# Tile 3 of the first block normalised and turned by DMA instead of TensorE, with the D-skip row and block 2 loaded later

## The chip, the cores and the metric

The kernel runs on one core of a Trainium2 chip. A core has TensorE (PE, matrix products into PSUM), VectorE (DVE), ScalarE (ACT), GpSimd (POOL), and SyncE (SP), which here only issues DMAs. Each engine works through its own list of instructions in order, and semaphores tie the lists together. DMAs issued by one engine form a queue; ACT issues a few as well. The metric is the device time of one execution in microseconds, lower is better.

## The reference

For x of 2048 rows and 512 columns (bf16), the reference computes a normalisation and adds two branches to x:

```
xn  = (x - mean(x)) / sqrt(var(x) + 1e-5)                 # per row
A   = 2 * Re(h C^T) + xn * Dskip,  h_t = Lam_bar * h_(t-1) + B_bar xn_t    # complex states, 512 of them
B   = (gelu(xn @ w_gate) * (xn @ w_up)) @ w_down          # 512 -> 1376 -> 512
out = x + A + B
```

## The kernel before

**Tiling.** The 2048 rows are four blocks of 512, each of four tiles of 128 rows. For a block the kernel normalises (LN), turns the normalised tiles so that the 512 columns lie on partitions (TR, one DMA transpose for a tile, into XNT), computes the hidden layer (GU, w_gate and w_up as stationary operands), the input of the states (BU), the recurrence on DVE (CHAIN, real scans after a rotation by cosine and sine tables), and the down projection with the states added (DN). SKIP makes xn * Dskip; it reads the normalised tile XN and the D-skip row DSKB. XN has eight places, so block 2's normalised tiles overwrite block 0's, behind SKIP(0).

**The start of block 0.** PE should not wait for four normalised and turned tiles, so the first 896 hidden columns of block 0 are computed in the other order: x turned as stationary operand, the weights moving. Tile by tile, x minus its mean (function cent for tiles 0 and 1, sub for 2 and 3) is turned by TensorE itself (cent_T: four transposes against an identity, evacuated by ACT into XC). Since the rows lie on partitions, the factor 1/sqrt(var) is applied in the evacuation: gelu with scale on ACT, product with scale on DVE (GT_evac). Units are pairs of a tile j and a column group u: FR = 0:256, 256:512, 512:768, 768:896, gate and up columns side by side in one PSUM bank. Tiles 0 to 2 with u = 0, 1 are accumulated in steps (GT_k), as the weights' first 512 columns arrive row block by row block; the other ten units, tile 3's four among them, are done whole (GT_mm), each four matmuls. The product H0 is turned by DMA later (H0_T). The last 480 columns go the usual way (GU(0, [7, 8, 9, 10]), the first of them in two halves, tiles 0 and 1, then 2 and 3); for that all four tiles are normalised again (norms) and turned by DMA (TR).

**Weights.** w_gate and w_up come in pieces: four row blocks of columns 0 to 512 (ld_wk), then columns 512 to 896 and 896 to 1376 as one DMA each (ld_w). A buffer list (WGc, WUc) gives one dependency for each piece; wdeps maps a group of 128 columns to its piece.

**Order.** PE and SP run in the order in which the program adds their operations. DVE, ACT and POOL are ordered by a list planner (Sched) from estimated durations, with some links that fix the order of two operations on one engine (order_behind; ch makes a chain of them). The first statistics of a later block come behind the last product of GT_evac on DVE. The SP queue is: loads of x and weights, the parameters' transpose (tr_par), TR of block 0, x of block 1, the two transposes of B (load_B, 3 us of issue each), in the same function the D-skip row and x of block 2, then TR of block 1, the transpose of block 0's last hidden columns, H0_T, TR of block 2, and so on.

**Waits named below.** GT_mm needs its weight pieces and its turned tile. GU(0) needs TR of block 0 and the weight tails. BU(1) begins with its first units in halves, which need tiles 0 and 1 of block 1. LN(2) needs x of block 2; SKIP(0) needs the D-skip row. DN(0) first adds the hidden layer of all four tiles, then the states, which need CHAIN(0) and C scaled on DVE (L595).

Of the kernel before, what the change touches and what calls it, by code (L numbers as in the profile page):

```python
# [9 lines left out]
ALU = mybir.AluOpType  # L10
# [351 lines left out]
def d_act(n, ptr=0): return 190.0 + 0.833 * n + 90.0 * ptr  # L362
# [3 lines left out]
def build(nc, ins, out):  # L366
    with ExitStack() as es:
        E = es.enter_context
        S = Sched(nc, es)
# [11 lines left out]
        assert WG.lo == 0 and WU.lo == WG.hi  # L381
        WGU = arena_t[:, 0:2 * KD * F].rearrange("p (w k f) -> p w k f", w=2, k=KD)
        WD = A.alloc("WD", [KF, D], BF16)
        FC = [(0, 512), (512, 896), (896, F)]
        WGc = [Buf("WGc%d" % i, "sbx", 10 * i, 10 * i + 1) for i in range(KD + 2)]
        WUc = [Buf("WUc%d" % i, "sbx", 100 + 10 * i, 101 + 10 * i) for i in range(KD + 2)]
        wdeps = lambda Wc, ft: Wc[0:KD] if ft < 4 else [Wc[KD + (ft > 6)]]
        WDc = [Buf("WDc%d" % i, "sbx", 200 + 10 * i, 201 + 10 * i) for i in range(2)]
        XNT_all = A.alloc("XNT", [NB, KD, TB_], BF16)
        XNT = ring(XNT_all, "XNT", NB)  # L390
# [97 lines left out]
            return S.dma(lambda e: e.dma_start(W.ap[:, k, f0:f1], src[128 * k:128 * (k + 1), f0:f1]),  # L488
                         256 * (f1 - f0), writes=[Wc[k]], tag="ld_w")

        def ld_w(W, Wc, src, n):
            f0, f1 = FC[n]
            return S.dma(lambda e: e.dma_start(W.ap[:, :, f0:f1], src[:, f0:f1].rearrange("(k p) f -> p k f", p=128)),
                         1024 * (f1 - f0), writes=[Wc[KD + n - 1]], tag="ld_w")

        def ld_x0(j, queue="sync", after=()):
            return S.dma(lambda e, j=j: e.dma_start(X[j].ap, x2[128 * j:128 * (j + 1), :]), 128 * 1024, writes=[X[j]], tag="ld_x0", queue=queue, after=after)  # L497
# [2 lines left out]
        for k in range(KD):  # L500
# [1 line left out]
                ld_x0(k)  # L502
            ld_wk(WG, WGc, ins["B_w_gate"], k)
            ld_wk(WU, WUc, ins["B_w_up"], k)
        ld_w(WG, WGc, ins["B_w_gate"], 1)
        ld_w(WU, WUc, ins["B_w_up"], 1)

        def load_par():
            for q, nm in enumerate(("A_log_dt", "A_Lambda_re", "A_Lambda_im")):
# [14 lines left out]
        def load_T(bufs, nms):  # L524
            for b_, nm in zip(bufs, nms):
                S.dma(lambda e, b_=b_, nm=nm: e.dma_start_transpose(b_.ap, ins[nm]),
                      1.4 * 512 * 1024, writes=[b_], tag="tr_" + nm, issue=3000.0)

        def load_W():
            ld_w(WG, WGc, ins["B_w_gate"], 2)  # L530
            ld_w(WU, WUc, ins["B_w_up"], 2)

        def load_B():
            load_T([A.sub(BBT_all, "BBTc%d" % c, c) for c in range(2)], ("A_B_re", "A_B_im"))
            S.dma(lambda e: e.dma_start(DSKB.ap, ins["A_Dskip"].unsqueeze(0).broadcast_to([128, D])),
                  128 * 1024, writes=[DSKB], tag="ld_dsk")
            ld_x(2)
# [166 lines left out]
        def GT_mm(j, u, bank):  # L704
            f0, f1 = FR[u]
            w = f1 - f0
            dst = PS[bank][:, 0:2 * w].rearrange("p (w f) -> p w f", w=2)

            def f(e):
                ins_ = None  # L710
                for k in range(KD):
                    ins_ = e.matmul(dst, XCd(j, k), WGU[:, :, k, f0:f1], start=(k == 0), stop=(k == KD - 1))  # L712
                return ins_
            PE(f, d_pe([2 * w] * KD), wdeps(WGc, 2 * u) + wdeps(WUc, 2 * u) + XCs[j], [BANK[bank]], "GT")

        def GT_evac(j, u, bank):
            f0, f1 = FR[u]
            w = f1 - f0
            GATE["nh"] = kk = (GATE["nh"] + 1) % 3
            sc, rb = rss[j]  # L720
            GATE["last_gelu"] = S.order_behind(ACT(lambda e: e.activation(GG[kk].ap[:, 0:w], PS[bank][:, 0:w], ACTF.Gelu_apprx_tanh, scale=sc),  # L721
                                                   d_act(w, 1), [BANK[bank], rb], [GG[kk]], "gelu"), GATE.get("last_gelu"))
            hp = Buf("H0_%d_%d" % (j, u), "sb", H0[j].lo + 2 * f0, H0[j].lo + 2 * f1)
            GATE["hm"] = S.order_behind(V(lambda e: e.scalar_tensor_tensor(H0[j].ap[:, f0:f1], PS[bank][:, w:2 * w], sc, GG[kk].ap[:, 0:w], ALU.mult, ALU.mult),  # L724
                                          d_dve_1x(w), [BANK[bank], GG[kk], rb], [hp], "hmul"), GATE.get("hm"))

        def H0_T():
            for j in range(4):
# [77 lines left out]
        def GU_rest(b):  # L806
            k2, ft = b % 2, KF - 1
            f0, m = 128 * ft, FROWS[ft]
            for i in range(2):
                bank = next_bank()  # L810

                def f(e, i=i, bank=bank):
                    ins_ = None
                    for j in (2 * i, 2 * i + 1):
                        dst = PS[bank][:, 256 * (j % 2):256 * (j % 2) + 2 * m].rearrange("p (w f) -> p w f", w=2)
                        for dk in range(KD):
                            ins_ = e.matmul(dst, XNT[b].ap[:, dk, 128 * j:128 * (j + 1)], WGU[:, :, dk, f0:f0 + m],  # L817
                                            start=(dk == 0), stop=(dk == KD - 1))
                    return ins_
                PE(f, d_pe([2 * m] * 8), [WGc[KD + 1], WUc[KD + 1]] + XTr(b), [BANK[bank]], "GR%d" % b)  # L820
                GATE["nh"] = kk = (GATE["nh"] + 1) % 3
                g_, u_ = (PS[bank][:, :].rearrange("p (j x) -> p j x", j=2)[:, :, w * m:(w + 1) * m] for w in range(2))
                gs, us = (t[kk].ap[:, 0:2 * m].rearrange("p (j f) -> p j f", j=2) for t in (GG, UPB))
                GATE["last_gelu"] = ACT(lambda e, g_=g_, gs=gs: e.activation(gs, g_, ACTF.Gelu_apprx_tanh),
                                        d_act(2 * m), [BANK[bank]], [GG[kk]], "gelu", after=GATE["before_gelu"])
                ACT(lambda e, u_=u_, us=us: e.activation(us, u_, ACTF.Copy), d_act(2 * m), [BANK[bank]], [UPB[kk]], "evU")
                V(lambda e, i=i, gs=gs, us=us: e.tensor_tensor(HR.ap[:, 2 * i:2 * i + 2, 0:m], gs, us, ALU.mult),
                  d_dve_tt2x(2 * m), [GG[kk], UPB[kk]], [HRp[i]], "hmul")
            S.dma(lambda e: e.dma_start_transpose(HTt[k2][ft].ap.rearrange("p (j t) -> p j t", j=4), HR.ap),
                  1.2 * 128 * 1024, reads=HRp, writes=[HTt[k2][ft]], tag="tr_h%d" % b, issue=1200.0)  # L830
# [161 lines left out]
        ch(*stats(0, 1))  # L992
        op, mn0, qb0, rq0 = root(0, 0, 3)
        ch(op)
        ch(*stats(0, 3)); ch(sub(3))
        ch(recip(qb0, rq0))
        op, mn3, qb3, rq3 = root(0, 3, 4)
        ch(op)
        rss = [(rq0.ap[:, i:i + 1], rq0) for i in range(3)] + [(rq3.ap, rq3)]
        for j in range(2):  # L1000
            ch(norms(0, [j], mn0, rq0, 0))
        ch(recip(qb3, rq3))
        TR(0, [0, 1])
        ks(1, 2, [0, 1])
        ks(2, 2, [0, 1])
        for j in range(3):
            GT_k(3, j, 0, [0, 1])
            if j == 0:
                cent_T(3, 0, 4, 6)
            GT_k(3, j, 1, [0, 1])  # L1010
            for u in range(2):
                GT_evac(j, u, acc(j, u))
        for (j, u), bank in zip([(3, 0), (3, 1), (0, 2), (0, 3), (1, 2), (1, 3), (2, 2), (2, 3), (3, 2), (3, 3)],
                                (6, 7, 0, 1, 2, 3, 4, 5, 0, 7)):
            GT_mm(j, u, bank)
            GT_evac(j, u, bank)
        rstate["n"] = 2
        norms(0, [2], mn0, rq0, 0)
        norms(0, [3], mn3, rq3, 3)
        TR(0, [2, 3])  # L1020
        ld_x(1)
        params()
        tables_dve(None)
        load_B()
        LN(1, [0, 1]); LN(1, [2, 3])
        TR(1)
        SKIP(0)
        GU(0, [7, 8, 9, 10], halved=[7])
        GATE["before_gelu"] = [tables_act([GATE["last_gelu"]])]
# [81 lines left out]
```

## Time and profile before

| | us |
|---|---|
| median of 3 runs | 176.86 |
| lowest and highest run | 176.77, 177.54 |
| the profiled execution's own time | 177.26 |
| its span (first to last instruction) | 175.9 |
| PE busy | 172.8 |
| DVE busy | 159.7 |
| ACT busy | 95.8 |

The span is what the trace shows; the execution's own time has 1.36 us more around it. PE's busy time counts pipelined matmuls by a modelled end, so neighbours overlap; distances from start to start tell the rate. TensorE's granted clock is 1.000 over the run. SPq and ACTq are the queues of issue instructions; a DMA's landing is the moment when its semaphore is complete.

### The profile page before, as it was taken

To read this page: it belongs to the slowest core of one execution; us is meant where nothing else is said; L and a number is where in the kernel's file an instruction comes from. 1 tells how busy PE (TensorE), PEld (TensorE's weight loads), DVE (VectorE), ACT (ScalarE), POOL (GpSimd) and SP (SyncE) were. 2 spreads that over 40 slices of the span, in tenths; PEclk is the share of its full clock that TensorE was granted. 3 is DMA by queue.
4 is the path that set the end of the run, shared out by engine and by line. 5 is a ranking of instruction groups with operands and counts; after the bars stand their busy time and mean duration, and the time that the engine had idled before them with its cause. 6 is when DMAs were issued, how large, how long until landed. Compare 5 with 4: busy or idle time off the path is not lost.

```text
span 175.9 us, 2549 instructions
## 1 busy us (share of the span) xinstructions
PE 172.8 (98%) x903; PEld 85.4 (49%) x903; DVE 159.7 (91%) x279; ACT 95.8 (54%) x187; POOL 10.7 (6%) x24
## 2 busy tenths in 40 slices
PE   7999999999999999999999999999999999999995
PEld 2645664744544444444644444444464444444454
DVE  6797999987999989889899999989999899999941
ACT  5367668999766899383676793000667970000000
POOL 3132120211000000002200000000000000000000
DMA  5999989975899000002015000002004000000311
GB/s 144 281 322 154 216 136 203 174 132 114 162 270 270 11 0 2 0 30 75 18 33 112 5 0 4 0 0 89 30 0 34 0 0 0 0 0 4 119 62 60
DMA packets 32421, 14.36 MB, mean 82 GB/s; under 512 B 23737, under 2 KB 32409, under 8 KB 32409
## 3 DMA queue, kind: packets, MB, share of 16 engines
q1 hardware_dynamic: 31952, 13.84, 36.9%
q10 hardware_dynamic: 456, 0.36, 0.6%
q8 instruction: 7, 0.11, 0.3%
q14 instruction: 6, 0.04, 0.1%
HBM read 6.46 MB, written 2.10 MB: 49 GB/s over the span
## 4 chain that ended last, share of the span: by engine, by line
PE 95%; DMA 2%; SPq 1%; issue 0%; DVE 0%
PE PS L885 37%; PE PS L843 32%; PE PS L749 16%; PE PS L712 4%; PE PS L817 3%; PE PS L701 2%; DMA arena<-in_B_w_up_dram 2%; SPq L488 1%; PE PS L684 0%; SPq L497 0%; DVE arena L903 0%
## 5 line engine op out<-in xcount | busy, mean ns | idle before, releaser
L885 PE MATMUL PS<-arena 128*128 128x512 bf16 (+3 forms) x323 | 66.2, 366 | 0.0
L843 PE MATMUL PS<-arena 128*128 128x512 bf16 (+1 forms) x272 | 58.1, 373 | 0.0
L885 PEld LDWEIGHTS PS<-arena 128*128 128x128 bf16 (+1 forms) x323 | 30.8, 98 | 35.2
L843 PEld LDWEIGHTS PS<-arena 128*128 128x128 bf16 x272 | 26.5, 98 | 29.5
L787 DVE TENSOR_TENSOR_SCAN arena<-arena 128x512 bf16<-128x512 f32 x32 | 38.9, 1256 | 0.0
L859 ACT ACTIVATE arena<-PS 128x512 bf16<-128x512 f32 x33 | 19.8, 599 | 26.2 <-DVE arena L903 16.7
L749 PE MATMUL PS<-arena 128*128 128x512 bf16 (+1 forms) x144 | 28.3, 355 | 0.1
L863 ACT ACTIVATE arena<-PS 128x512 bf16<-128x512 f32 x33 | 19.8, 599 | 5.4 <-PE PS L843 5.4
L749 PEld LDWEIGHTS PS<-arena 128*128 128x128 bf16 x144 | 14.0, 98 | 13.7 <-DMA arena<-arena 0.6
L877 ACT ACTIVATE PS<-arena 128x512 f32<-128x512 bf16 (+2 forms) x17 | 9.6, 582 | 19.7 <-DVE arena L903 19.0
L758 ACT ACTIVATE arena<-PS 128x512 bf16<-128x512 f32 x32 | 17.6, 597 | 1.6 <-PE PS L749 1.6
L903 DVE TENSOR_TENSOR arena<-PS,arena 128x512 bf16<-128x512 f32 (+2 forms) x17 | 10.9, 654 | 6.4 <-PE PS L885 6.4
L865 DVE TENSOR_TENSOR arena<-arena 128x512 bf16<-128x512 bf16 x33 | 13.2, 419 | 2.1 <-ACT arena L863 2.0
L776 DVE TENSOR_TENSOR arena<-arena 128x4096 bf16<-128x4096 bf16 (+1 forms) x5 | 9.2, 1859 | 0.4 <-ACT arena L611 0.4
L799 DVE TENSOR_TENSOR arena<-arena 128x4096 bf16<-128x4096 bf16 x4 | 9.2, 2291 | 0.1
L774 DVE TENSOR_TENSOR arena<-arena 128x4096 bf16<-128x4096 bf16 (+1 forms) x5 | 9.2, 1861 | 0.0
L800 DVE TENSOR_TENSOR arena<-arena 128x4096 bf16<-128x4096 bf16 x4 | 9.1, 2287 | 0.0
L615 DVE BATCH_NORM_STATS2 arena<-arena 128x6 f32<-128x512 bf16 x12 | 7.8, 685 | 0.9 <-DMA arena<-in_A_x_dram 0.7
L721 ACT ACTIVATE arena<-PS,arena 128x256 bf16<-128x256 f32 (+1 forms) x16 | 6.5, 450 | 3.3 <-DVE arena L621 1.5
L712 PE MATMUL PS<-arena 128*128 128x512 bf16 (+1 forms) x40 | 7.1, 336 | 0.0
L701 PE MATMUL PS<-arena 128*128 128x256 bf16 (+1 forms) x36 | 6.2, 308 | 0.2 <-DMA arena<-in_B_w_up_dram 0.2
L724 DVE SCALAR_TENSOR_TENSOR arena<-PS,arena 128x256 bf16<-128x256 f32 (+1 forms) x16 | 6.2, 444 | 0.0
(95 smaller groups left out, 124.2 us busy)
## 6 DMA issues: line engine op xcount, KB each, us to landing
out_dram<-arena SPq DMA_DIRECT2D x15, 128.0 KB, 1.7
arena<-in_A_x_dram SPq DMA_DIRECT2D x3, 512.0 KB, 6.3
arena<-in_B_w_down_dram SPq DMA_DIRECT2D x1, 1280.0 KB, 8.8
arena<-in_B_w_gate_dram SPq DMA_DIRECT2D x4, 128.0 KB, 3.4
arena<-in_B_w_up_dram SPq DMA_DIRECT2D x4, 128.0 KB, 3.6
arena<-in_B_w_gate_dram SPq DMA_DIRECT2D x1, 480.0 KB, 6.8
arena<-in_B_w_up_dram SPq DMA_DIRECT2D x1, 480.0 KB, 7.6
arena<-arena SPq DMA_TRANSPOSE x25, 3.3
```

What stands on the lines that cost most here:

```text
L701: PE(lambda e: e.matmul(dst, XCd(j, k), WGU[:, ws[0]:ws[-1] + 1, k, f0:f1], start=first, stop=k == KD - 1, skip_group_check=True), d_pe([w ...
L712: ins_ = e.matmul(dst, XCd(j, k), WGU[:, :, k, f0:f1], start=(k == 0), stop=(k == KD - 1))
L749: ins_ = e.matmul(PS[bank][:, 128 * j0:128 * j1], BBT[c][dk].ap[:, 128 * s:128 * (s + 1)], XNT[b].ap[:, dk, 128 * j0:128 * j1], start=(dk ...
L758: GATE["evBu"] = ACT(lambda e, bank=bank, k3=k3, s=s, c=c: e.activation(SSc[k3][s][c].ap, PS[bank][:, :], ACTF.Copy), d_act(512), [BANK[ba ...
L787: V(lambda e, g=g, rb=rb, init=init: e.tensor_tensor_scan(g.ap, rb, g.ap, init, ALU.mult, ALU.add), d_dve_scan(512), [g, PA[RRr]] + ([CARc ...
L843: ins_ = e.matmul(PS[bank][0:m, c0:c1], W.ap[:, dk, 128 * ft:128 * ft + m], XNT[b].ap[:, dk, c0:c1], start=(dk == 0), stop=(dk == KD - 1))
L859: GATE["last_gelu"] = ACT(lambda e, bg=bg, kk=kk, m=m: e.activation(GG[kk].ap[0:m, :], PS[bg][0:m, :], ACTF.Gelu_apprx_tanh), d_act(512), ...
L863: ACT(lambda e, bu=bu, kk=kk, m=m: e.activation(UPB[kk].ap[0:m, :], PS[bu][0:m, :], ACTF.Copy), d_act(512), [BANK[bu]], [UPB[kk]], "evU")
L865: V(lambda e, kk=kk, m=m, ft=ft, k2=k2: e.tensor_tensor(HTt[k2][ft].ap[0:m, :], GG[kk].ap[0:m, :], UPB[kk].ap[0:m, :], ALU.mult), d_dve_tt ...
L877: ACT(lambda e: e.activation(PS[bank][:, c0:c1], X[tt].ap[:, c0:c1], ACTF.Copy), d_act(c1 - c0), [X[tt]], [BANK[bank]], "seed")
L885: ins_ = e.matmul(PS[bank][:, c0:c1], l_[:, 128 * j:128 * (j + 1)], r_[:, c0:c1], start=False, stop=last and n == len(ops) - 1, skip_group ...
L903: V(lambda e: e.tensor_tensor(OUTB[ko].ap[:, c0:c1], PS[bank][:, c0:c1], XD[tt].ap[:, c0:c1], ALU.add), d_dve_1x(c1 - c0), [BANK[bank], XD ...
```

## The change

- Tile 3 of block 0 is no longer centred by DVE (sub), turned by TensorE (cent_T) and evacuated by ACT. It is normalised in full (norms) and turned by DMA with the others, and its four units read XNT; gelu and product have no scale.
- TR of block 0 has the order 0, 3, 1 and then 2, instead of 0, 1 and then 2, 3.
- The whole units' order is (0,2), (1,2), (2,2), (0,3), (1,3), (2,3) and then tile 3's four; before, it began with (3,0), (3,1) and went on tile by tile, tile 3's last two at the end. PSUM banks are assigned anew.
- Weight columns 512 to 896 come as two pieces, 512 to 768 and 768 to 896, for w_gate and w_up each. The tail of w_up is issued by ACT behind the last eviction of a turned tile, not by SP.
- The D-skip row and x of block 2 are issued behind TR of block 1 instead of ahead of it.

```diff
-        FC = [(0, 512), (512, 896), (896, F)]
+        FC = [(0, 512), (512, 768), (768, 896), (896, F)]
...
-        wdeps = lambda Wc, ft: Wc[0:KD] if ft < 4 else [Wc[KD + (ft > 6)]]
+        wdeps = lambda Wc, ft: Wc[0:KD] if ft < 4 else [Wc[KD + (ft > 5) + (ft > 6)]]
...
-        ld_w(WG, WGc, ins["B_w_gate"], 1)
-        ld_w(WU, WUc, ins["B_w_up"], 1)
+        for n in (1, 2):
+            ld_w(WG, WGc, ins["B_w_gate"], n)
+            ld_w(WU, WUc, ins["B_w_up"], n)
...
         def load_W():
-            ld_w(WG, WGc, ins["B_w_gate"], 2)
-            ld_w(WU, WUc, ins["B_w_up"], 2)
+            ld_w(WG, WGc, ins["B_w_gate"], 3)
 
         def load_B():
             load_T([A.sub(BBT_all, "BBTc%d" % c, c) for c in range(2)], ("A_B_re", "A_B_im"))
+
+        def load_skip():
             S.dma(lambda e: e.dma_start(DSKB.ap, ins["A_Dskip"].unsqueeze(0).broadcast_to([128, D])),
                   128 * 1024, writes=[DSKB], tag="ld_dsk")
             ld_x(2)
...
-                    ins_ = e.matmul(dst, XCd(j, k), WGU[:, :, k, f0:f1], start=(k == 0), stop=(k == KD - 1))
+                    xs = XCd(j, k) if j < 3 else XNT[0].ap[:, k, 128 * j:128 * (j + 1)]
+                    ins_ = e.matmul(dst, xs, WGU[:, :, k, f0:f1], start=(k == 0), stop=(k == KD - 1))
...
+            if j < 3:
+                sc, rb = rss[j]
+                fg = lambda e: e.activation(g, gate, ACTF.Gelu_apprx_tanh, scale=sc)
+                fh = lambda e: e.scalar_tensor_tensor(h, up, sc, g, ALU.mult, ALU.mult)
+                rb = [rb]
+            else:
+                fg = lambda e: e.activation(g, gate, ACTF.Gelu_apprx_tanh)
+                fh = lambda e: e.tensor_tensor(h, up, g, ALU.mult)
+                rb = []
...
-        ch(*stats(0, 3)); ch(sub(3))
-        ch(recip(qb0, rq0))
+        S.order_behind(ld_w(WU, WUc, ins["B_w_up"], 3, "scalar"), GATE["evTA"])
+        ch(*stats(0, 3))
         op, mn3, qb3, rq3 = root(0, 3, 4)
         ch(op)
-        rss = [(rq0.ap[:, i:i + 1], rq0) for i in range(3)] + [(rq3.ap, rq3)]
-        for j in range(2):
-            ch(norms(0, [j], mn0, rq0, 0))
+        ch(recip(qb0, rq0))
+        rss = [(rq0.ap[:, i:i + 1], rq0) for i in range(3)]
+        ch(norms(0, [0], mn0, rq0, 0))
+        ch(norms(0, [1], mn0, rq0, 0))
         ch(recip(qb3, rq3))
-        TR(0, [0, 1])
+        ch(norms(0, [3], mn3, rq3, 3))
+        TR(0, [0, 3, 1])
         ks(1, 2, [0, 1])
         ks(2, 2, [0, 1])
         for j in range(3):
             GT_k(3, j, 0, [0, 1])
-            if j == 0:
-                cent_T(3, 0, 4, 6)
             GT_k(3, j, 1, [0, 1])
             for u in range(2):
                 GT_evac(j, u, acc(j, u))
-        for (j, u), bank in zip([(3, 0), (3, 1), (0, 2), (0, 3), (1, 2), (1, 3), (2, 2), (2, 3), (3, 2), (3, 3)],
-                                (6, 7, 0, 1, 2, 3, 4, 5, 0, 7)):
+        for (j, u), bank in zip([(0, 2), (1, 2), (2, 2), (0, 3), (1, 3), (2, 3), (3, 0), (3, 1), (3, 2), (3, 3)],
+                                (6, 7, 0, 1, 2, 3, 4, 5, 6, 7)):
             GT_mm(j, u, bank)
             GT_evac(j, u, bank)
-        rstate["n"] = 2
+        rstate["n"] = 0
         norms(0, [2], mn0, rq0, 0)
-        norms(0, [3], mn3, rq3, 3)
-        TR(0, [2, 3])
+        TR(0, [2])
         ld_x(1)
         params()
         tables_dve(None)
         load_B()
         LN(1, [0, 1]); LN(1, [2, 3])
         TR(1)
+        load_skip()
         SKIP(0)
         GU(0, [7, 8, 9, 10], halved=[7])
```

More of the change, by code (lines that the diff above doesn't have):

```diff
@@ L383, in build @@
         WD = A.alloc("WD", [KF, D], BF16)
-        FC = [(0, 512), (512, 896), (896, F)]
-        WGc = [Buf("WGc%d" % i, "sbx", 10 * i, 10 * i + 1) for i in range(KD + 2)]
-        WUc = [Buf("WUc%d" % i, "sbx", 100 + 10 * i, 101 + 10 * i) for i in range(KD + 2)]
-        wdeps = lambda Wc, ft: Wc[0:KD] if ft < 4 else [Wc[KD + (ft > 6)]]
+        FC = [(0, 512), (512, 768), (768, 896), (896, F)]
+        WGc = [Buf("WGc%d" % i, "sbx", 10 * i, 10 * i + 1) for i in range(KD + 3)]
+        WUc = [Buf("WUc%d" % i, "sbx", 100 + 10 * i, 101 + 10 * i) for i in range(KD + 3)]
+        wdeps = lambda Wc, ft: Wc[0:KD] if ft < 4 else [Wc[KD + (ft > 5) + (ft > 6)]]
         WDc = [Buf("WDc%d" % i, "sbx", 200 + 10 * i, 201 + 10 * i) for i in range(2)]
@@ L489, in ld_wk, with ld_w @@
                          256 * (f1 - f0), writes=[Wc[k]], tag="ld_w")
-        def ld_w(W, Wc, src, n):
+        def ld_w(W, Wc, src, n, queue="sync"):
             f0, f1 = FC[n]
             return S.dma(lambda e: e.dma_start(W.ap[:, :, f0:f1], src[:, f0:f1].rearrange("(k p) f -> p k f", p=128)),
-                         1024 * (f1 - f0), writes=[Wc[KD + n - 1]], tag="ld_w")
+                         1024 * (f1 - f0), writes=[Wc[KD + n - 1]], tag="ld_w", queue=queue)
         def ld_x0(j, queue="sync", after=()):
@@ L711, in f @@
                 for k in range(KD):
-                    ins_ = e.matmul(dst, XCd(j, k), WGU[:, :, k, f0:f1], start=(k == 0), stop=(k == KD - 1))
+                    xs = XCd(j, k) if j < 3 else XNT[0].ap[:, k, 128 * j:128 * (j + 1)]
+                    ins_ = e.matmul(dst, xs, WGU[:, :, k, f0:f1], start=(k == 0), stop=(k == KD - 1))
                 return ins_
-            PE(f, d_pe([2 * w] * KD), wdeps(WGc, 2 * u) + wdeps(WUc, 2 * u) + XCs[j], [BANK[bank]], "GT")
+            PE(f, d_pe([2 * w] * KD), wdeps(WGc, 2 * u) + wdeps(WUc, 2 * u) + (XCs[j] if j < 3 else [XT0[j]]), [BANK[bank]], "GT")
         def GT_evac(j, u, bank):
@@ L719, in GT_evac @@
             GATE["nh"] = kk = (GATE["nh"] + 1) % 3
-            sc, rb = rss[j]
-            GATE["last_gelu"] = S.order_behind(ACT(lambda e: e.activation(GG[kk].ap[:, 0:w], PS[bank][:, 0:w], ACTF.Gelu_apprx_tanh, scale=sc),
-                                                   d_act(w, 1), [BANK[bank], rb], [GG[kk]], "gelu"), GATE.get("last_gelu"))
             hp = Buf("H0_%d_%d" % (j, u), "sb", H0[j].lo + 2 * f0, H0[j].lo + 2 * f1)
-            GATE["hm"] = S.order_behind(V(lambda e: e.scalar_tensor_tensor(H0[j].ap[:, f0:f1], PS[bank][:, w:2 * w], sc, GG[kk].ap[:, 0:w], ALU.mult, ALU.mult),
-                                          d_dve_1x(w), [BANK[bank], GG[kk], rb], [hp], "hmul"), GATE.get("hm"))
+            gate, up, g, h = PS[bank][:, 0:w], PS[bank][:, w:2 * w], GG[kk].ap[:, 0:w], H0[j].ap[:, f0:f1]
+            if j < 3:
[7 more added lines that the diff above has]
+                rb = []
+            GATE["last_gelu"] = S.order_behind(ACT(fg, d_act(w, 1), [BANK[bank]] + rb, [GG[kk]], "gelu"), GATE.get("last_gelu"))
+            GATE["hm"] = S.order_behind(V(fh, d_dve_1x(w), [BANK[bank], GG[kk]] + rb, [hp], "hmul"), GATE.get("hm"))
         def H0_T():
@@ L819, in f @@
                     return ins_
-                PE(f, d_pe([2 * m] * 8), [WGc[KD + 1], WUc[KD + 1]] + XTr(b), [BANK[bank]], "GR%d" % b)
+                PE(f, d_pe([2 * m] * 8), [WGc[KD + 2], WUc[KD + 2]] + XTr(b), [BANK[bank]], "GR%d" % b)
                 GATE["nh"] = kk = (GATE["nh"] + 1) % 3
```

## The prediction, put on record before the result

> **What bounds the kernel now.** I read the page's busy times first, then the chain of waits, then the timeline of TensorE (PE), of the DMA queue of SyncE (SPq) and the DMA rates around the edited stretch.
>
> ```profile
> PE 172.8 (98%) x903; PEld 85.4 (49%) x903; DVE 159.7 (91%) x279; ACT 95.8 (54%) x187; POOL 10.7 (6%) x24
> ...
> PE 95%; DMA 2%; SPq 1%; issue 0%; DVE 0%
> ```
>
> PE is busy for 172.8 of 175.9 us and carries 95% of the chain. So the change can win only PE time or a PE wait, and any new PE wait is paid in full. PE in the edited stretch (start, duration, line):
>
> ```profile
> 7.70 2.05 PE L701 MATMUL PS<-arena 128*128 128x256 bf16 x9
> 9.69 0.40 PE L684 MATMUL PS<-arena 128*128 128x128 bf16 x4
> 9.92 1.24 PE L701 MATMUL PS<-arena 128*128 128x512 bf16 x5
> 11.00 7.09 PE L712 MATMUL PS<-arena 128*128 128x512 bf16 x40
> 17.93 5.36 PE L843 MATMUL PS<-arena 128*128 128x256 bf16 x32
> ```
>
> L684 at 9.69 is the turning of tile 3. L712 is the ten units of GT_mm: six of 4x512 columns (u = 0, 1, 2) and four of 4x256 (u = 3). Their starts are 0.865 and 0.435 us apart, and 6 x 0.865 + 4 x 0.435 = 6.93 = 17.93 - 11.00, so they run without a gap. The chain's only stall behind the start-up is this:
>
> ```profile
> 31.52 0.12 issue
> 31.64 7.11 PE PS L749 x48
> ```
>
> That is BU(1), which waits for the turned tiles of block 1. Then SyncE's queue:
>
> ```profile
> 5.47 0.43 SPq L493 DMA_DIRECT2D arena<-in_B_w_gate_dram  x1
> 5.95 0.51 SPq L493 DMA_DIRECT2D arena<-in_B_w_up_dram  x1
> 6.50 0.51 SPq L493 DMA_DIRECT2D arena<-in_B_w_gate_dram  x1
> 7.04 0.65 SPq L493 DMA_DIRECT2D arena<-in_B_w_up_dram  x1
> 7.82 1.99 SPq L515 DMA_TRANSPOSE arena<-arena  x1
> 10.27 5.15 SPq L736 DMA_TRANSPOSE arena<-arena  x4
> ...
> 23.07 0.58 SPq L535 DMA_DIRECT2D arena<-in_A_Dskip_dram  x1
> 23.69 0.43 SPq L482 DMA_DIRECT2D arena<-in_A_x_dram  x1
> 24.17 6.34 SPq L736 DMA_TRANSPOSE arena<-arena  x4
> ```
>
> The landings, asked for one at a time, are 10.22, 11.95, 13.27 and 14.63 for the four L493 loads, 15.01 for L515, and 15.22, 15.65, 16.16 and 16.65 for the four turns at 10.27. The first turn is issued at 10.27 but lands only behind the last weight load. The queue is worked off in order, and its engines are full (columns: PE, PEld, DVE, ACT, POOL busy, clock, DMA share, GB/s):
>
> ```profile
> 5.00:6.00 1.00, 1.00 (x11) 0.69 (x8) 0.33 (x2) 0.49 (x1) 0.00 (x0) 1.00 0.98 331
> 9.00:10.00 1.00, 1.00 (x9) 0.45 (x8) 0.86 (x6) 0.15 (x1) 0.84 (x3) 1.00 0.99 290
> 12.00:13.00 1.00, 1.00 (x7) 0.44 (x5) 1.00 (x4) 0.72 (x2) 0.00 (x0) 1.00 1.28 362
> ```
>
> The trace's packet records give one engine's time per packet (medians): 256 bytes 18 ns, 768 bytes 36, 960 bytes 44, 1024 bytes 46.
>
> **Part 1: no turn on PE.** PE loses the four transposes (9.92 - 9.69 = 0.23 us) and the 0.10 it idled for DVE before them (the L701 matmul at 9.37 takes 0.22, so 9.59 to 9.69). GT_mm can begin at 11.00 - 0.33 = 10.67. DVE loses one subtraction of 0.35 and ACT one eviction of 0.59, both beside PE. The scale-free gelu and product keep their shapes, and I cost them at nothing: ACT and DVE follow PE there.
>
> **Part 2: the first weight piece.** GT_mm now opens with (0,2), which needs w_up columns 512 to 768. Before, columns 512 to 896 were first read by (0,2) at 12.73 and had landed at 11.95. 512-byte packets do not occur here; between 18 and 36 ns I take the line's 27. Then this piece lands after 27/36 of the 3.18 us that the two old loads took behind the load that landed at 8.77, so at 8.77 + 2.39 = 11.16 (18 and 36 give 10.36 and 11.95). With the ACT queue's share (part 3) it may be 0.7 later. So (0,2) waits some 0.5 to 1.2 us. As long as part 3 holds this costs nothing, since the six units in front of tile 3 (3 x 0.865 + 3 x 0.435 = 3.90) then end at 15.1 to 15.8. If part 3's wait is gone, this is what remains.
>
> **Part 3: tile 3 turned by DMA.** Its four units come last; without waits (3,0) would start at 10.67 + 3.90 = 14.57. Its turn is the second on the queue, behind tile 0, where the second turn landed at 15.65 before. I take the engines as full until then, so work ahead of it is time. The pieces of 512 and 256 bytes replace each 768-byte packet by two: 1024 x (27 + 18 - 36) ns / 16 engines = +0.58 us (0 to 1.15 with 512 bytes at 18 to 36). The w_up tail of 480 KB goes to ACT's queue. ACT is idle from 8.39, when tile 2's last eviction ends, to 9.85, so the issue (0.65 by its SP row) fits there and holds up no gelu. ACT's x load issued at 1.00 had its first packet at 2.24, so this one's come from about 9.7, far ahead of the turn. The move saves the SP queue work of 1024/2 x 44 ns / 16 = 1.41 us, but the same 16 engines do it in the same time: with both queues running from 2 to 3 us they moved 329 GB/s, with one from 5 to 6 us 331. So tile 3 lands at 15.65 + 0.58 = 16.23. Ends: 14.82 if the ACT load took nothing from the SP queue (-1.41), 16.80 if 512 bytes cost 36 ns. PE starts about 0.04 behind a landing (6.28 and 6.32 for L701), so (3,0) starts at 16.27.
>
> The Trainium skill ("DMA: Bandwidth & Descriptors", "Issuing engines are not separate DMA queues") says that DMAs started by several engines share the same 16 DMA engines and save only issue time. By that rule the sum keeps its +0.58; were the ACT queue an engine of its own, it would be rival B's.
>
> SP's issues do not gate this: one load more ahead of L515 puts it at about 8.4, the turns at 10.4, 11.7, 13.0 and 14.2. Tile 3's normalisation, done before at 11.39 to 11.80, is in time for 11.7 within 0.1. A turn with an empty queue lands 2.5 us after issue, so up to 13.7 nothing changes. L515 lands 0.58 later; behind it stand POOL's power (L557) and the tables on DVE, read by ACT only from 30 us on. The DMA issue on ACT delays only what follows it there, and that starts at 9.85.
>
> Behind (3,0) PE holds (3,1), (3,2), (3,3) and all of GU(0), whose start is 16.27 + 3 x 0.865 + 0.435 = 19.30 against 17.93: **+1.37 us**. Tile 2's turn, last, lands near 17.2, and both weight tails before 16.2, in time for 19.3.
>
> **Part 4: D-skip row and x of block 2 behind the turns of block 1.** Two issues (1.1 us) leave the queue ahead of four turns, of which the first two landed at 31.19 and 31.55. They now land sooner, while BU(1) comes 1.37 later: the 0.12 stall goes (**-0.12**). What is late next is the moved pair. LN(1) stays behind the last product on DVE, so the fourth turn is issued near 26.8, D-skip at 28.1, x at 28.7. x took 6.27 before and 4.06 for block 1, so it lands at 32.8 to 35.0. LN(2) began at 30.76 and would begin at 32.1 with the shift. DVE may idle up to 2.9; I take 1 to 2, hidden because DN(0) first reads DVE's results at 73.6 and the last of them ended at 71.9: 1.7, to which PE's 1.37 adds. Later blocks have 3 us or more (the last states begin at 164.7, their last product ends at 161.7).
>
> **Sum.** +1.37 - 0.12 = +1.25 us on a span of 175.9. The profiled execution took 177.26, so it would take 178.5; it lies 0.40 above the median of 176.86 (runs 176.77 to 177.54), against which I forecast **178.1**. A change of 0.5% is 0.88 us, about what a measurement can tell from none.
>
> **Rivals.**
> A, the forecast: tile 3's turn waits behind the weights. Own range 177.7 to 178.7 (landing 15.86 to 16.80).
> B: ACT's load does not delay the turn, because it is issued late or fits in gaps. Tile 3 lands at 14.82, and the first piece's 0.5 decides: (3,0) at 10.67 + 0.5 + 3.90 = 15.07, GU(0) at 18.10, +0.17 - 0.12 = +0.05: 176.9. For it: engines each had stalled packets of 0.8 to 1.6 us that another queue might fill. Against it: share 0.98 to 1.28 already.
> C, on the other side: the change does what it says, both the piece and the turn in time: -0.33 - 0.12 = -0.45: 176.4. It needs the piece by 10.67 and the turn by 14.53; the rows put them at 11.16 and 16.23. Even this is within 0.5%.
> D: x of block 2 past its cover. Landing at 35.0 or behind, with DVE's order fixed, LN(2) is 2.9 late, and with a queue of turns as at 23 us another 2: 4.9 - 1.7 - 1.37 leaves 1.8 at DN(0)'s states, 179.9; it decides from 3.1 us of DVE delay on. Against it: D-skip products and the table products can fill the hole.
> E: the 256-byte pieces cost twice their row, 36 ns: 1024 x 18 / 16 = 1.15 more, tile 3 at 17.38, 179.3. Against it: the 256-byte rows of the parameters, loaded on ACT's queue near 3 us, took 18 ns. The Trainium skill ("DMA: Bandwidth & Descriptors", "Specifications") has under 512 bytes a read-modify-write, the case E; the trace's rows bear out only 14 bytes per ns against 21.
>
> **How the numbers follow.** A 0.58, B 0.21, C 0.08, D 0.06, E 0.07. The range leaves out C and D and reaches to B's low side and to E: 176.6 to 179.3. Slower by over 0.5% (from 177.7): most of A, D, E and little of B, 0.65. Faster by over 0.5% (below 176.0) has no case, only what I overlook: 0.04. Within: 0.31.
>
> **What would show it.** No L684 near 9.7 and L712 from 10.7 or somewhat later; a PE gap inside L712 ended by a DMA into the arena, before its 25th matmul; L843 at about 19.3; no stall at BU(1); the second L736 turn landing near 16.2. The forecast is wrong if that turn lands before 15.8 or if DVE, not PE, moves the end.

## The result and the profile after

The changed kernel takes 178.72 us (median of 9, 177.60 to 179.54) against 177.05 us (median of 9, 176.73 to 177.57). The ratio is 1.0082, with a 95% interval of 1.0063 to 1.0101: slower, as forecast. Two later measurements of the same kernel, each beside the kernel before, gave 1.0035 (1.0014 to 1.0055) and 1.0037 (1.0024 to 1.0051). So the sign stands, and the size moves between sessions from about 0.6 to about 1.5 us.

The page's busy times and chain of the changed kernel (lines of its own listing: L703 is GT_k, L715 GT_mm, L853 the GU matmuls, L759 BU, L746 the block turns):

```profile
PE 172.2 (97%) x884; PEld 86.1 (49%) x899; DVE 159.4 (90%) x278; ACT 94.2 (53%) x186; POOL 15.3 (9%) x24
...
PE 87%; ACT 2%; DMA 2%; issue 1%; DVE 0%
```

PE is still the bound, but now a DMA of 2% of the span stands in the chain behind the start-up. In TensorE's timeline (start, duration, line; in brackets the idle time before it and what ended it):

```profile
10.79 4.06 PE L715 MATMUL PS<-arena 128*128 128x512 bf16 x24
15.88 3.20 PE L715 MATMUL PS<-arena 128*128 128x512 bf16 x16 [1.02 <-DMA arena<-arena]
18.91 5.36 PE L853 MATMUL PS<-arena 128*128 128x256 bf16 x31
```

The 24 matmuls of tiles 0 to 2 run without a gap from 10.79. Then PE stands still until 15.88. Its last matmul before that started at 14.58 and takes 0.11 to the next one, so the gap is 1.19 us (the bracket has 1.02, because it counts from the modelled end). GU(0) begins at 18.91 instead of 17.93. What ended the gap is the second L746 turn, tile 3's. Its own view:

```profile
L746 SPq DMA_TRANSPOSE arena<-arena x1: 1265/1265/1265, 11.9 to 11.9; - x1
...
  PEld PS L715: 1.3, 1
  PE PS L715: 1.0, 1
...
DMA to landing us min/median/max: 3.9/3.9/3.9
```

Issued at 11.89, it landed at 15.83, behind the weight tails (14.36 and 14.74). In the chain of waits of the changed kernel (start, length, engine and line) the same is one piece:

```profile
11.89 3.94 DMA arena<-arena
15.83 0.05 issue
15.88 3.20 PE PS L715 x16
```

Everything behind GU(0) follows it at a fixed distance. In the profiled executions the span minus the start of GU(0) is 157.96 us in the kernel before and 157.76, 157.76 and 157.74 in the three of the changed kernel (175.89 - 17.93, 176.67 - 18.91, 176.04 - 18.28, 176.09 - 18.35). The kernel before has 0.2 more there because of its stall at BU(1): its L749 matmuls at 31.14 and 31.64 are 0.50 apart instead of 0.22, so that stall was 0.28 us. It is gone in the changed kernel. (Steps of 0.43 us, at 20 to 50 matmul intervals, are matmul records missing from the trace and no waits: the page counts 884 matmuls and 899 weight loads, so 15 of 899 are missing here.)

### The profile page after: what moved, and what is told of

The parts are those of the page before. It is cut to its first block, busy times and chain, and to the rows that moved or that the text cites. A ratio compares the mean times of both kernels' runs of the same rounds, so it can differ in the third digit from the quotient of the medians.

```text
span 176.7 us, 2528 instructions
## 1 busy us (share of the span) xinstructions
PE 172.2 (97%) x884; PEld 86.1 (49%) x899; DVE 159.4 (90%) x278; ACT 94.2 (53%) x186; POOL 15.3 (9%) x24
## 4 chain that ended last, share of the span: by engine, by line
PE 87%; ACT 2%; DMA 2%; issue 1%; DVE 0%
PE PS L895 37%; PE PS L853 32%; PE PS L759 13%; PE PS L827 3%; DMA arena<-arena 2%; PE PS L715 2%; ACT arena L768 1%; ACT arena L612 1%; DVE arena L728 0%; DVE arena L913 0%
## 5 line engine op out<-in xcount | busy, mean ns | idle before, releaser
L853 PE MATMUL PS<-arena 128*128 128x512 bf16 (+1 forms) x265 | 57.3, 373 | 0.4
L853 PEld LDWEIGHTS PS<-arena 128*128 128x128 bf16 x272 | 26.6, 98 | 29.4
L759 PE MATMUL PS<-arena 128*128 128x512 bf16 (+1 forms) x142 | 28.1, 355 | 0.1
L759 PEld LDWEIGHTS PS<-arena 128*128 128x128 bf16 x144 | 14.1, 98 | 13.3
L875 DVE TENSOR_TENSOR arena<-arena 128x512 bf16<-128x512 bf16 x33 | 13.2, 418 | 1.1 <-ACT arena L873 1.0
L715 PE MATMUL PS<-arena 128*128 128x512 bf16 (+1 forms) x40 | 7.3, 337 | 1.0 <-DMA arena<-arena 1.0
L673 DVE TENSOR_TENSOR arena<-arena 128x512 bf16<-128x512 bf16 x16 | 6.0, 421 | 2.0 <-DMA arena<-in_A_Dskip_dram 2.0
L562 POOL TENSOR_TENSOR arena<-arena 128x4 f32<-128x4 f32 x1 | 6.6, 6642 | 3.1 <-DVE arena L561 3.1
L703 PE MATMUL PS<-arena 128*128 128x256 bf16 (+1 forms) x36 | 6.3, 323 | 0.0
```

Of the source, the lines that this page charges most:

```text
L715: ins_ = e.matmul(dst, xs, WGU[:, :, k, f0:f1], start=(k == 0), stop=(k == KD - 1))
L759: ins_ = e.matmul(PS[bank][:, 128 * j0:128 * j1], BBT[c][dk].ap[:, 128 * s:128 * (s + 1)], XNT[b].ap[:, dk, 128 * j0:128 * j1], start=(dk ...
L853: ins_ = e.matmul(PS[bank][0:m, c0:c1], W.ap[:, dk, 128 * ft:128 * ft + m], XNT[b].ap[:, dk, c0:c1], start=(dk == 0), stop=(dk == KD - 1))
L875: V(lambda e, kk=kk, m=m, ft=ft, k2=k2: e.tensor_tensor(HTt[k2][ft].ap[0:m, :], GG[kk].ap[0:m, :], UPB[kk].ap[0:m, :], ALU.mult), d_dve_tt ...
```

## Experiments

Theory T: the loss is the wait for tile 3's turn, which lands when the DMA engines have done what reached them before. Theory D: D-skip row and x of block 2 come so late that DVE makes DN(0) wait. Times are medians beside the kernel before on the same chip; ratios have their 95% interval. Part 4 undone (its first run), part 4 alone and the two runs with both tails on one queue behind the pieces ran together; the others ran in two groups on another chip.

**Part 4 undone.**

```diff
         load_B()
+        load_skip()
         LN(1, [0, 1]); LN(1, [2, 3])
         TR(1)
-        load_skip()
```

> Part 4 undone: D-skip row and x of block 2 ahead of the turns of block 1 again, all else as in the changed kernel. Theory T (the whole loss is tile 3's turn landing behind the weights; the executions differ by when it lands): GU(0) still starts near 18.9 us, BU(1) waits 0.0 to 0.3 us for block 1's turns, so the time stays within 0.3 us of the changed kernel, 178.5 to 179.0. Theory D (in many executions the late x of block 2 delays DVE past DN(0)'s states, where the profile of the changed kernel shows C's last scaling end at 74.2 and the states begin at 74.3): the last scaling ends 2 us earlier, the spread shrinks and the time falls by 0.5 to 1.0 us, to 177.7 to 178.2.

Measured: 177.55 against 177.03, 1.0031 (1.0014 to 1.0047). At that time this looked like theory D, 1.2 us below the changed kernel's 178.72. But the trace did not bear it out: tile 3's turn landed at 15.69, GU(0) started at 18.77, and span minus that start is 157.74, the same as with part 4. In this execution (0,2) also waited 0.59 us for the first piece, which landed at 11.06. So the two had to be measured side by side.

**The changed kernel again, and part 4 undone beside it.** The same two programs on another chip, the changed kernel in two groups.

> The changed kernel itself once more, for a second trace and more executions beside the runs below. Theory D: the end follows the slack of DN(0)'s states, so if this profiled execution is a long one (178.5 us or more), its trace shows TensorE idle ahead of the states of DN(0) until C's last scaling ends, by the amount that its span is over 176.7 us beyond any longer wait for tile 3. Theory T: the extra is in front of (3,0), inside GT_mm, and DN(0) shows no idle time.

> The changed kernel a third time, now beside part 4 undone on the same chip. In its two profiles so far tile 3's turn landed at 15.83 and 15.20 us and GU(0) started at 18.91 and 18.28, for spans of 176.7 and 176.0: theory T says that the landing alone makes this spread, so span minus the start of GU(0) is 157.7 to 157.8 again, whatever the time. Theory D says that in an execution of 178.5 us or more DN(0)'s states wait for DVE, so that this difference comes out larger, by up to 1 us.

> Part 4 undone, once more, beside the changed kernel. Theory D: its median is 0.5 us or more below the changed kernel's on this chip. Theory T: within 0.3 us of it, on either side (it loses BU(1)'s stall of at most 0.3 us and nothing else).

Measured: the changed kernel 177.56 (177.12 to 178.56) against 176.90, 1.0035 (1.0014 to 1.0055), and 177.44 against 176.84, 1.0037 (1.0024 to 1.0051). Part 4 undone, beside the second: 177.38, 1.0036 (1.0023 to 1.0048). So part 4 is worth nothing measurable either way, and theory D falls for these executions. The 1.2 us of before is a difference between sessions, not between the kernels. The profiled executions were of 177.34 and 177.44 us, so the expectation for one of 178.5 or more was not put to the test. TensorE's timeline of the third execution, where the turn landed at 15.27:

```profile
10.65 4.06 PE L715 MATMUL PS<-arena 128*128 128x512 bf16 x24
15.31 3.20 PE L715 MATMUL PS<-arena 128*128 128x512 bf16 x16 [0.60 <-DMA arena<-arena]
18.35 2.99 PE L853 MATMUL PS<-arena 128*128 128x256 bf16 x21
```

The gap is 0.77 us here (14.43 + 0.11 to 15.31), and GU(0) is 0.56 earlier than in the first execution (18.91). The spans differ by 0.58. In the second execution the turn landed at 15.20, but GT_mm itself began late, at 11.20, so only about 0.14 us of standing was left; GU(0) still follows the landing. In part 4 undone, beside it, the turn landed at 15.12 and GU(0) began at 18.20.

The landing sets the time. In seven traced executions with this start (three of the changed kernel, two of part 4 undone, and the two below with both tails on one queue) the execution's own time is the landing of tile 3's turn plus 162.13 to 162.18 us.

**Part 4 alone, on the kernel before.**

```diff
         def load_B():
             load_T([A.sub(BBT_all, "BBTc%d" % c, c) for c in range(2)], ("A_B_re", "A_B_im"))
+
+        def load_skip():
             S.dma(lambda e: e.dma_start(DSKB.ap, ...
...
         TR(1)
+        load_skip()
```

> The kernel before with part 4 alone: D-skip row and x of block 2 behind the turns of block 1. Theory T: the stall of 0.28 us at BU(1) goes and nothing takes its place, 176.8 (ratio 0.998 to 0.999). Theory D: DVE waits 2 to 4 us for the pair, the C scaling that ended at 71.9 ends near 74 and DN(0)'s states, due at 73.3, wait up to 0.9 us: 177.0 to 177.8 (ratio 1.000 to 1.004).

Measured: 177.19 against 177.03, 1.0004 (0.9989 to 1.0018). Block 1's first turns landed at 25.55 and 27.57 instead of 31.19 and 31.55; BU(1) has no gap, and span minus the start of GU(0) is 157.68, which is 0.28 less than before. The profiled execution lost most of that at the start, where a w_up row block came late (GU(0) at 18.11). C's last scaling ended at 71.47, 2.0 us ahead of DN(0)'s states, so theory D is refused here as well. The 0.28 is in the trace but too small for the times to show.

**Both tails on SP.**

```diff
         def load_W():
             ld_w(WG, WGc, ins["B_w_gate"], 3)
+            ld_w(WU, WUc, ins["B_w_up"], 3)
...
-        S.order_behind(ld_w(WU, WUc, ins["B_w_up"], 3, "scalar"), GATE["evTA"])
```

> The tail of w_up goes back to the SP queue, ahead of the parameters' transpose, all else as in the changed kernel. Forecast A (both queues share full DMA engines, so work ahead of the turn is time wherever it was issued): tile 3's turn lands near 15.8 as in the changed kernel (within 0.3) and the time is within 0.3 us of it. Rival B (a load on ACT's queue costs the SP queue little): the turn lands up to 1.4 us later, near 17.2, and the time rises by up to 1.4 us, to about 180.

Measured: 178.38 (177.52 to 180.70) against 177.03, 1.0067 (1.0041 to 1.0093). TensorE's timeline:

```profile
10.66 4.06 PE L716 MATMUL PS<-arena 128*128 128x512 bf16 x24
16.34 3.20 PE L716 MATMUL PS<-arena 128*128 128x512 bf16 x16 [1.62 <-DMA arena<-arena]
19.37 0.82 PE L854 MATMUL PS<-arena 128*128 128x256 bf16 x6
```

The turn landed at 16.29, against 15.69 with w_up's tail on ACT's queue on the same chip (part 4 undone). That lies between the two expectations (A allowed 0.3 us, B named up to 1.4). But these are single executions, and five with one tail on ACT's queue (three of the changed kernel, two of part 4 undone) landed from 15.12 to 15.83. The DMA rates show where this execution lost its time (columns as in the prediction):

```profile
12.00:13.00 1.00, 1.00 (x6) 0.44 (x5) 1.00 (x4) 1.00 (x3) 0.00 (x0) 1.00 1.09 368
13.00:14.00 1.00, 1.00 (x9) 0.78 (x8) 1.00 (x3) 0.98 (x4) 0.00 (x0) 1.00 2.87 175
14.00:15.00 1.00, 0.72 (x7) 0.39 (x4) 0.85 (x3) 0.86 (x4) 0.00 (x0) 1.00 0.07 23
```

From 14 to 15 us the DMA engines moved almost nothing. In the packet records one of the tails' 960-byte packets, started at 11.00, took 1.32 us instead of 44 ns. From 13.5 to 14.8 only 33 more of them started, which is about what one engine does at 44 ns each (an estimate). And 20 of the 256-byte packets of the transposes behind them, started between 13.2 and 14.0, all ended between 15.05 and 15.11. So, as I read it, most engines stood at their first transposing packets until the slowest one had done its weights.

The same is seen in all eleven traces in which the turns stand behind both tails, the two without the new pieces included: the last 960-byte packet ends somewhere between 13.6 and 14.8 us, and the second turn lands 1.43 to 1.66 us after that. So the 0.60 goes with how far one engine lagged, and that the move to another queue brought it about is not shown. The medians of the two kernels, 178.38 and 177.55, have ratio intervals that just overlap; a gain from the move is possible.

**Both tails on ACT's queue.**

```diff
         def load_W():
-            ld_w(WG, WGc, ins["B_w_gate"], 3)
+            pass
...
+        S.order_behind(ld_w(WG, WGc, ins["B_w_gate"], 3, "scalar"), GATE["evTA"])
         S.order_behind(ld_w(WU, WUc, ins["B_w_up"], 3, "scalar"), GATE["evTA"])
```

> Both weight tails on ACT's queue, so that on the SP queue only the pieces up to column 896 stand ahead of the turns. If what holds the turn is the order of its own queue, it lands 2.5 us after its issue at 11.9 plus some of the shared engines' time, 14.4 to 15.0; the wait in front of (3,0) falls from 1.2 to at most 0.4 us and the time by 0.8 to 1.2 us, to 177.5 to 177.9. If the shared engines alone set it, whichever queue the tails are on, the turn stays at 15.8 and the time at 178.7. Theory D adds: with PE earlier and DVE not, DN(0)'s states wait for DVE, and the gain comes out up to 0.8 us smaller.

Measured: 177.85 against 177.03, 1.0040 (1.0024 to 1.0055). The SP queue's last weight piece landed at 11.44, and nothing but turns was left on it. Still tile 3's turn landed at 15.62:

```profile
L746 SPq DMA_TRANSPOSE arena<-arena x1: 1346/1346/1346, 11.0 to 11.0; - x1
...
DMA to landing us min/median/max: 4.6/4.6/4.6
```

The tails on ACT's queue, issued at 8.13 and 8.56, landed at 13.30 and 14.77; the parameters' transpose, issued on SP at 7.71, landed at 14.93, and the turns behind it. The packet records show 960-byte packets of ACT's queue and almost no others from 11.0 to 11.5 us. So an empty queue of its own did not help the turn. It comes behind the weight loads, whichever queue they came from.

**Both tails later, on ACT's queue.** Part 4 undone, the tails taken from their old places and put behind the fourth gelu, the following gelus behind them.

```diff
         for j in range(3):
             GT_k(3, j, 0, [0, 1])
             GT_k(3, j, 1, [0, 1])
             for u in range(2):
                 GT_evac(j, u, acc(j, u))
+                if (j, u) == (1, 1):
+                    tl = S.order_behind(ld_w(WG, WGc, ins["B_w_gate"], 3, "scalar"), GATE["last_gelu"])
+                    GATE["last_gelu"] = S.order_behind(ld_w(WU, WUc, ins["B_w_up"], 3, "scalar"), tl)
```

> Part 4 undone as in the first experiment, and both weight tails issued by ACT behind the fourth gelu, near 12.2 us, so that they reach the DMA engines behind tile 3's turn. If the turn waits for work that reached the shared engines before it: tile 3 lands near 14 us instead of 15.7, (3,0) waits at most 0.2 us, L853 starts at 17.6 to 18.0 unless the tails, landing near 17.2, hold it; the time falls by 0.8 to 1.2 us against part 4 undone alone (177.55) to 176.4 to 176.8, with BU(1)'s stall of 0.3 to 0.6 us as what is late next. If turns are slow for another reason (a fixed time until they start), tile 3 still lands at 15.5 or later and the time stays at 177.4 to 177.7.

Measured: 178.59 against 176.90, 1.0094 (1.0080 to 1.0109), a miss. Tile 0's turn, issued at 9.98, landed at 12.43, in 2.45 us. Tile 3's, issued at 11.25, landed at 16.50, though the first tail was issued only at 11.69:

```profile
L746 SPq DMA_TRANSPOSE arena<-arena x1: 1266/1266/1266, 11.2 to 11.2; - x1
...
  PEld PS L715: 1.5, 1
  PE PS L715: 1.2, 1
...
DMA to landing us min/median/max: 5.2/5.2/5.2
```

The tails landed at 16.30 and 18.50, and tile 1's turn at 18.76. Nearly all of tile 3's packets had started by 13.6 us in the packet records, so most of the delay is between the data and the semaphore. The Trainium skill ("DMA: Bandwidth & Descriptors", "Queues, rings and completion order") says that a DMA's semaphore write on an engine lands only after every earlier write of that engine, across its queues. The trace agrees: the turns landed 0.2 to 0.3 us behind each tail, and in the packet records 32 packets of 4 bytes on SP's queue, which close tile 3's turn as I read them, started between 14.73 and 15.98 us, each within 0.02 us of one of 16 such packets on ACT's queue. But no run here isolates this cause.

**The same, with D-skip row and x of block 2 on ACT's queue.** The two loads of load_skip have queue="scalar", behind the last gelu of GT_mm, and load_skip stands behind load_B.

> As the kernel with late tails, and the D-skip row and x of block 2 on ACT's queue behind the last gelu of GT_mm (near 18.6 us), so that neither stands ahead of block 1's turns on the SP queue nor behind them. Expected: BU(1)'s stall goes (0.3 to 0.6 us) and DVE has x of block 2 by 27 us, so that DN(0)'s states keep 1.5 us or more of slack: 176.2 to 176.6, faster than the kernel before by 0.2 to 0.5%. Against it: the loads take 1.8 us of the engines ahead of B's second transpose, and BU(0) may wait for it up to 0.5 us.

Measured: 178.91 against 176.90, 1.0114 (1.0098 to 1.0131). The start fails in the same way (tile 3's turn at 16.32, GU(0) at 19.40). The second half did what was expected of it, to no use: span minus GU(0)'s start is 157.76, C's last scaling ends at 71.79 with the states at 74.8.

**Both tails on SP, between the turns.**

```diff
-        TR(0, [0, 3, 1])
+        TR(0, [0, 3])
+        ld_w(WG, WGc, ins["B_w_gate"], 3)
+        ld_w(WU, WUc, ins["B_w_up"], 3)
+        TR(0, [1])
```

(load_W and the line for ACT's queue are without the tails.)

> The changed kernel with both weight tails on the SP queue between the turns of tiles 3 and 1, nothing on ACT's queue, part 4 kept. If a turn only waits for what reached the engines before it, tile 3 lands at 13.7 to 14.0 us, in time for (3,0) at 14.6; the tails land near 15.5 and 16.8, tiles 1 and 2 near 17.3 and 17.8; GU(0) starts at 17.6 to 17.9 and BU(1) has no stall: 176.2 to 176.7 (ratio 0.996 to 0.999). If the tails come too late, the wait moves to GU(0), up to 0.8 us, and the time is 177.0 to 177.5. With theory D, DN(0)'s states add up to 0.5 us.

Measured: 177.87 against 176.84, 1.0063 (1.0051 to 1.0075). Tile 3's turn now lands 2.5 us after its issue, at 13.78, as expected, and GT_mm has no gap at all:

```profile
11.65 6.44 PE L715 MATMUL PS<-arena 128*128 128x512 bf16 x37
19.09 3.20 PE L853 MATMUL PS<-arena 128*128 128x256 bf16 x22 [0.99 <-DVE arena L732]
```

But the wait is in front of GU(0), 1.16 us from 17.93 to 19.09. The view names DVE, whose last L732 ended at 18.89; but the weight loader stood from 14.71 to 18.75 at an instruction that waits for tile 1's turn, and that landed at 18.72, behind the tails at 16.6 and 18.0. So at most the last 0.3 us can be anything else. Putting tile 3 first moves the wait to the next consumer, and the delay was larger than the 0.8 allowed for. This order also left the DMA engines little to do: they moved 58 to 133 GB/s in each microsecond from 10 to 14, where the changed kernel moved 166 to 356; the tails were issued only at 12.61 and 13.24.

**Part 1 undone, first try.** Part 4 undone; cent_T(3, 0, 4, 6) put back at its old place, with sub(3), tile 3's scale and XC as operand.

> Part 4 undone, and tile 3 centred and turned on TensorE as before the change, its units still last, the pieces, the order and ACT's load kept. Part 1 alone is missing. Forecast A: the wait in front of (3,0) (0.5 to 1.2 us) goes and the turn (0.33 us) comes back; what stays is the first piece's wait of 0 to 0.6 us. GU(0) starts at 17.9 to 18.5, the time is 0.3 to 0.8 us below part 4 undone alone (177.55): 176.8 to 177.3. If tile 3's turn is not the cause, the time stays at 177.5 or rises by the turn's 0.33.

Measured: 181.43, 1.0280 (1.0248 to 1.0312). This tests nothing of part 1: the full normalisation of tile 3, left where the change has it, comes ahead of the turn and overwrites the centred tile. TensorE turned the normalised tile (it waited for it until 11.25), and its units were then scaled twice, so tile 3's hidden columns are not the reference's.

**Part 1 undone.** As above, but with the old order of turns and the normalisation of tile 3 behind GT_mm.

```diff
-        ch(*stats(0, 3))
+        ch(*stats(0, 3)); ch(sub(3))
...
-        ch(norms(0, [3], mn3, rq3, 3))
-        TR(0, [0, 3, 1])
+        TR(0, [0, 1])
...
             GT_k(3, j, 0, [0, 1])
+            if j == 0:
+                cent_T(3, 0, 4, 6)
...
-        TR(0, [2])
+        norms(0, [3], mn3, rq3, 3)
+        TR(0, [2, 3])
```

> Part 1 alone undone (with part 4 undone as well): tile 3 is centred, turned on TensorE and evacuated by ACT as before, its four units still come last, the pieces, the unit order and ACT's load of w_up's tail are kept, and the DMA turns come in the old order. Theory T: no wait in front of (3,0), at most 0.3 us in front of (0,2) for the first piece, GU(0) starts at 17.9 to 18.2, the time is 176.8 to 177.3 (ratio 0.999 to 1.002), below part 4 undone with the DMA turn (ratio 1.003). If the order or the pieces were the cause, it stays at a ratio of 1.003 or more.

Measured: 177.30 (176.93 to 178.31) against 176.84, 1.0039 (1.0020 to 1.0058). The profiled execution is of 176.95 us and agrees with theory T: no gap in front of tile 3's units, GU(0) at 17.89, span 175.64.

```profile
9.43 0.40 PE L686 MATMUL PS<-arena 128*128 128x128 bf16 x4
9.66 1.24 PE L703 MATMUL PS<-arena 128*128 128x512 bf16 x5
10.81 7.24 PE L715 MATMUL PS<-arena 128*128 128x512 bf16 x40
17.89 3.42 PE L853 MATMUL PS<-arena 128*128 128x256 bf16 x23
```

The median does not agree: the ratio is as large as with the DMA turn. The profiled execution is among the shortest of twelve, and the long ones have no trace. So the pieces, the unit order or ACT's load may cost something in them, too. The first piece is one place where that could be: here (0,2) started at 10.81, 0.13 us behind its landing at 10.68, and that landing went from 10.22 to 11.06 in the traces of the kernels tried. With the turn out of the way, a late piece would delay PE directly. But that it did is not shown, and so the loss of this kernel's median stays open. No version tried here beats the kernel before.

## Why the prediction came out right, and where its sizes were off

**What bounds the kernel.** Right: a new PE wait was paid in full, and span minus the start of GU(0) stayed the same to 0.1 us in every trace of a kernel with this change in it.

**Part 1.** Right: no turn on PE, GT_mm from 10.79 (10.65 and 11.20 in the other two traces) against a forecast of 10.67. In the execution with 11.20 PE was late by 0.4 already at tile 2's turning.

**Part 2.** The 512-byte packets took 27 ns, as read off the line. The wait of 0.5 to 1.2 us for the first piece was too large: it landed at 10.51 to 10.65 in the changed kernel, not at 11.16 or later. As the prediction said, this costs nothing while tile 3 is later.

**Part 3.** The mechanism is right: the turn waits behind the weights, PE starts 0.05 behind the landing, and GU(0) is late. The size was too large: forecast 16.23 and +1.37 at GU(0), measured 15.83, 15.20 and 15.27, and +0.98, +0.35 and +0.42. By the prediction's own sign (wrong if the turn lands before 15.8) two of the three executions are against it.

The term that failed is the +0.58 for the smaller pieces. It was worked out from medians, 27 + 18 against 36 ns. The means, which hold the stalled packets as well, are 47 to 50 ns for the two packets against 44 to 45 for the one. And with both tails on SP, where nothing but the pieces differs ahead of the tails, the last piece landed at 11.43, while the undivided ones landed at 11.95 in the kernel before and 11.54 with part 4 alone. That the turn of that run landed at 16.29, near the 15.65 + 0.58 of the sum, is chance: its trace shows one packet of 1.32 us and an engine that lagged.

The sum also took the engines as full until the turn. They are not: in the changed kernel the rate falls from 356 GB/s between 12 and 13 us to 166 and 147 in the next two (362, 215 and 172 in the kernel before). There the turn waits for the slowest engine, and that differs by 0.7 us between executions of one start. The move of w_up's tail to ACT's queue, costed at no gain, is not refused by this: by 13.0 us the engines had moved 3.32 to 3.34 MB in the changed kernel and 3.33 MB with both tails on SP. That agrees with the rule of the Trainium skill that was weighed there ("DMA: Bandwidth & Descriptors", "Issuing engines are not separate DMA queues": issue time is all that another queue saves).

**Part 4.** Right that BU(1)'s stall goes. Its size was 0.28, not 0.12: the chain counts from modelled matmul ends, and starts would have shown it. Right that the late x is hidden, but barely in the first trace: DVE waited 2.0 us for the D-skip row and 0.6 for x of block 2, C's last scaling ended at 74.20, and the states begin at 74.3. In the other two traces about 0.7 and 0.5 us of slack were left (72.96 and 73.19 against states from about 73.65 and 73.73). The prediction expected 1 to 2 us of idle time, at most 2.9; it was 2.6, 2.2 and 2.1.

**The sum.** +1.25 forecast, +1.45 in the result on record (0.82% of 177.05; the medians are 1.67 apart), about +0.6 in the two repeats. The profiled execution was at +0.78 of span, which is 0.98 - 0.28 and 0.08 at the end. That the recorded time lies so near the forecast is in part luck: the terms of the sum came out smaller, and the long executions that bring the median back up have no trace. What made those of 178.5 to 179.5 us is open. A later landing would do it (by the 162.15 us above, one of 178.72 would need a landing near 16.6, an estimate), and so would DN(0)'s vanishing slack.

**Rivals.** C did not happen. B is not borne out: no turn landed near its 14.82. D is refused in the traces and by the pair on one chip. E is refused: 256-byte pieces took 18 ns.

## What to carry to other kernels

Before a step is moved from a full compute engine to a DMA, add up all that the DMA engines must finish ahead of it, whichever queue it was issued on, and compare that with when the engine runs out of other work: here the work lasted to about 14.6 us, and a turn that stood second behind both weight tails landed at 15.1 or later in every trace. Count with mean packet times and with the slowest of the engines: the medians made a cost of 0.58 us that was not there, and the landing moved by 0.7 us between executions. Another order can move the wait from one consumer to the next, as the tails between the turns did. Compare a kernel whose time hangs on a landing only with one measured beside it: the same program gave 1.0082, 1.0035 and 1.0037.

## What the runs showed of the hardware that was not expected

DMA transposes that stood behind plain loads did not get through before the slowest engine had done its loads: in eleven traces the second of two such transposes landed 1.43 to 1.66 us after the last weight packet ended, whether that was at 13.6 or at 14.8.

A DMA transpose on the SP queue landed only behind a plain load of ACT's queue issued after it (issued at 11.25 and landed at 16.50, 0.2 us behind a load issued at 11.69; in a second kernel with late tails 11.28, 16.32 and 11.72), while with the same loads behind it on its own queue it landed in 2.5 us.

GpSimd's power on 128x4 elements took 6.64 us in the changed kernel instead of 1.01, and the first scan waited 0.73 for it (the same two figures stand in the other two traces of this kernel):

```profile
43.49 6.64 POOL L562 TENSOR_TENSOR arena<-arena 128x4 f32<-128x4 f32 x1 [3.13 <-DVE arena L561]
```

```profile
45.94 0.69 DVE L788 TENSOR_TENSOR arena<-arena 128x1024 bf16<-128x1024 bf16 x1
...
50.17 1.22 DVE L797 TENSOR_TENSOR_SCAN arena<-arena 128x512 bf16<-128x512 f32 x1 [0.73 <-POOL arena L562]
```

In the kernel before it ran from 39.04, when DVE had nothing to do from 39.03 to 39.48. In the changed kernel DVE went from one two-input bf16 operation to the next over most of that time, until 49.4. That fits what the Trainium skill says of one SBUF port pair that DVE and GpSimd hold in turn ("SBUF — State Buffer", "SBUF: two separate sides"); the duration on GpSimd is a rough one.
